# The low part of q padded with zero rows, so that both score matmuls of a head have 128 rows of weights

## The chip, the cores and the metric

The kernel runs on one core of one Trainium2 chip. The metric is device time in microseconds, the median of several runs. Three engines' names recur below: TensorE (PE in the profile) does matmuls and transposes, VectorE (DVE) and ScalarE (ACT) do elementwise work and read PE's results from the eight PSUM banks, GpSimd (POOL) does elementwise work on SBUF, and SyncE (SP) issues most DMAs.

## What is computed

Three layers in float32, one after the other, over 2304 tokens (4 sequences of 576) of 512 features:

```python
# attention: 8 heads of 64, each query sees its own and the 63 keys before it
scores = np.matmul(q, k.transpose(0, 1, 3, 2)) / np.sqrt(64)
rel = pos[:, None] - pos[None, :]
scores = np.where((rel >= 0) & (rel < 64), scores, -1e9)
attn = softmax(scores)                       # exp of scores less their maximum, over the sum + 1e-9
x = np.matmul(attn, v)                       # then [tokens, 512]
# feed-forward: d_ff 1536
xn = x / np.sqrt(np.mean(x * x, -1) + 1e-6) * rms_g
g = xn @ w_gate
x = (g * sigmoid(g) * (xn @ w_val)) @ w_out
# mixture of 8 experts, one for each token: 512 -> 1024 -> 512
e = argmax(x @ r_gate);  gate, eom = softmax(x @ r_gate)[e], sigmoid(x @ r_eom)[e]
out = gate * eom * (relu(x @ w1[e]) @ w2[e])
```

## The kernel before

**Numbers in two parts.** TensorE runs in a fast float32 form that rounds its operands. To keep precision every operand is split into a rounded part and the rest ("high" and "low", written by the helpers `hi_i` and `lo_i`, for q with its scale by `scaled_hi` and `scaled_lo`), and a product is the sum of high x high, high x low and low x high, accumulated in one bank. So a feed-forward step has three matmuls for each block of weights (lines 1117 to 1119 for gate and value, 1159 to 1161 for the output).

**Tiles and stages.** The tokens are 18 tiles of 128. For a tile, `attention_front` loads q, k and v, turns q and k with TensorE (line 578) and splits them; `attention_tile` computes the scores in two halves of four heads, adds the mask on VectorE (line 775), takes the maximum (787), the exponential on ScalarE (791), normalises (`nm`: 808 on ScalarE, else 357), turns the probabilities with TensorE (824), multiplies with v (880), and normalises the rows. The feed-forward layer takes the tiles in six groups (of 4, 2, 3, 3, 3 and 3 tiles); in the plan the attention of one group stands beside the feed-forward work of the group before. The experts follow at the end.

**What sets the order.** Each operation is given to a planner (`Plan`) with its engines' estimated costs, what it reads and writes, and a due time (`prio`). Its list scheduling picks for each engine the next operation and, where several engines could do it, the engine. It also models TensorE's clock: work of a low weight `rows` counts less towards keeping it up. The outcome is one fixed order for every engine; a cost that is changed can so move other instructions.

**Scores of the later tiles.** From tile 7 on (`K["stk"]`, 11 tiles), q and k are stacked. A head has 64 features, and heads go in pairs: head 2i lies in partitions 0 to 63 and head 2i+1 in partitions 64 to 127 of what the transposes leave. For the heads of one parity j, `stack(qb, j)` is a block of 128 partitions with the high part of q twice, and `stack(kt, j)` one with the high part of k in the half that is the head's own and the low part in the other. One matmul of 128 rows (line 758) so gives high x high and high x low together. The remaining low x high is a second matmul into the same columns of the bank (line 759) that uses only the head's own 64 partitions of both operands. The low part of q stands in the third block of `q_all`, even heads in the upper half of the partitions, odd heads in the lower. An operation (`mm`) does two heads, hence four matmuls of 192 columns; a tile has four of them, 16 matmuls, and the 11 tiles 176.

**Tile 0 to 6** use another form (`mmz`, lines 729 to 731): q is laid out with zeros, all its matmuls have 128 rows, and `q_all` is filled with zeros once at the start (line 562).

Of the kernel before, what the change touches and what calls it, by code (L numbers as in the profile page):

```python
# [9 lines left out]
F32 = mybir.dt.float32  # L10
# [29 lines left out]


class Buf:
    """An instance of a tag's tile: it takes one of the tag's slots from its first operation to its last."""

    def __init__(self, tag=None, t=None):
        self.tag, self.t, self.slot = tag, t, None
# [11 lines left out]


class Filler:  # L60
    """Work that keeps the tensor engine's clock up while it has none of its own."""

    def __init__(self, fn, lo):
        self.fn, self.lo = fn, lo


class Plan:
    """Operations with what they read and write, put in an order for every engine by list scheduling."""

    def __init__(self):  # L70
        self.ops, self.tags, self.ordered, self.newest, self.gates = [], {}, {}, {}, []
# [43 lines left out]
    def order(self):  # L115
# [21 lines left out]
        ticks = {}  # L137

        def pe_time(at, c, rows):
            """PE's time for c us of work at the full clock: a tick runs at half of it unless the one before was busy"""  # L140
            t0 = at
            while c > 1e-9:
                n = int(at / TICK + 1e-9)
                rate = 1.0 if ticks.get(n - 1, 0.0) >= FULL else 0.5
                step = min(c / rate, (n + 1) * TICK - at + 1e-9)
                c -= step * rate
                at += step
                ticks[n] = ticks.get(n, 0.0) + step * rate * rows
            return at - t0
# [18 lines left out]
        while left:  # L168
            while wait and wait[0][0] <= now + 1e-9:
                t, _, e, o = heapq.heappop(wait)  # L170
# [99 lines left out]
def attention_ffn_moe(  # L270
# [115 lines left out]
            yield done, step, b, s  # L386
            done += step

# [1 line left out]
    tag("t2k", "r", 2, [P, XW])  # L390
    ident = fixed("ident", [P, P])
    ones = fixed("ones", [P, 2])
# [16 lines left out]
        )  # L409

    def c_masks(e):
        """rows: 64 queries, twice; columns: their window's 128 keys; variants: inside, at the start of a batch, inside, inside"""
        nc.gpsimd.memset(masks.t, 0.0)
        for j in range(2):
            m = masks.t[64 * j:64 * j + 64]
            nc.gpsimd.affine_select(
                out=m, in_=m, compare_op=ALU.is_gt, fill=NEG, base=0, pattern=[[0, 4], [1, P]], channel_multiplier=-1
            )
            nc.gpsimd.affine_select(
                out=m, in_=m, compare_op=ALU.is_ge, fill=NEG, base=64, pattern=[[0, 4], [-1, P]], channel_multiplier=1  # L420
            )
        nc.gpsimd.memset(masks.t[:, 1, 0:64], NEG)
# [46 lines left out]
        nc.sync.dma_start(out=rw.t[:, :, E:2 * E], in_=r_eom.rearrange("(k p) e -> p k e", p=P))  # L469


# [1 line left out]
    tag("bank", "ps", 8, [P, 512])  # L473
    tag("raw", [("r", 3), ("mr", 3)], 0, [P, 2 * DM], I32)
    tag("rx", "a", 4, [P, DM])
# [35 lines left out]
    for us in GROUPS:  # L511
        GT.append(GT[-1] + PP * sum(SIZES[u] for u in us))

# [1 line left out]
    attn_ops = []  # L515

    def bank():
# [7 lines left out]
    xn_w, xn_r = [[] for _ in SIZES], [[] for _ in SIZES]  # L525

    def vt(t):
        """where tile t's attention stands in the plan"""
        g = GROUP[UNIT[t][0]]
        if g == 0:  # L530
            return t * K["stag"]
        first = FT[GROUPS[g][0]]
        n = FT[GROUPS[g][-1] + 1] - first
        return GT[g - 1] + (t - first) * (GT[g] - GT[g - 1]) / n * K["span"] - K["lead"]
# [8 lines left out]
        return go  # L543

    def low(t, bk, b, h, l, prio, sc=False):
        """what the rounded parts (b, 0) leave of the bank, into (b, 1)"""
        def v():
            return bk.t.rearrange("p (i t) -> p i t", t=P)

        pl.op(  # L550
            cost(512, "lp"), lambda e: (scaled_lo if sc else lo_i)(e, l(), v(), h()), r=[bk, (b, 0)], w=[(b, 1)],
            prio=prio,
        )

    kt_b = {}
    qb = Buf(None, q_all[:, 0:3 * DM].rearrange("p (z i t) -> p z i t", z=3, i=4))
    qz = q_all.rearrange("p (z i c t) -> p z i c t", z=2, i=4, c=2)

    def zeros(e):
# [7 lines left out]
    def attention_front(t):  # L567
# [21 lines left out]
            return slice(64 * j, 64 * j + 64)  # L589

        def stack(b, j, w=None):
            """the block of the heads of parity j in a stacked tile, as [partitions, pairs, columns]"""
            n = 192 if w else P
            a = b.t[:, 0:2].rearrange("p z i t -> p (z i t)").rearrange("p (i j t) -> p i j t", j=2, t=n)[:, :, j]
            return a[:, :, w] if w else a

        if t < K["qzt"]:
            for j in range(2):
                def own(z, j=j):
                    return qz[half(j), z, :, :, half(j)]  # L600

                def turned(bk=bk, j=j):
                    return bk.t[half(j)].rearrange("p (i c t) -> p i c t", i=4, c=2)

                pl.op(
                    cost(512, "hp"), lambda e, own=own, turned=turned: scaled_hi(e, own(0), turned()),
                    r=[bk], w=[(qb, (j, 0))], prio=pr,
                )
                pl.op(
                    cost(512, "lp"), lambda e, own=own, turned=turned: scaled_lo(e, own(1), turned(), own(0)),  # L610
                    r=[bk, (qb, (j, 0))], w=[(qb, (j, 1))], prio=pr,
                )
        elif not stk:
            pl.op(cost(512, "hp"), lambda e, bk=bk: scaled_hi(e, qb.t[:, 0], view(bk)), r=[bk], w=[(qb, 0)], prio=pr)
            low(t, bk, qb, lambda: qb.t[:, 0], lambda: qb.t[:, 1], pr, sc=True)
        else:
            for j in range(2):
                a, z = half(j), half(1 - j)
                pl.op(
                    cost(512, "hp"), lambda e, bk=bk, j=j, a=a: scaled_hi(e, stack(qb, j)[a], view(bk)[a]),  # L620
                    r=[bk], w=[(qb, (j, 0))], prio=pr,
                )
                pl.op(
                    cost(512, "hs"), lambda e, j=j, a=a, z=z: hi_i(e, stack(qb, j)[z], stack(qb, j)[a]),
                    r=[(qb, (j, 0))], w=[(qb, (j, 1))], prio=pr, lock="pv",
                )
                pl.op(
                    cost(512, "lp"), lambda e, bk=bk, j=j, a=a: scaled_lo(e, qb.t[a, 2], view(bk)[a], stack(qb, j)[a]),
                    r=[bk, (qb, (j, 0))], w=[(qb, (j, 2))], prio=pr,
                )  # L630
        bk2 = bank()
# [48 lines left out]
    def attention_tile(t, kt, rv, stack):  # L680
# [30 lines left out]
        for hf in range(2):  # L711
# [36 lines left out]
            for j in range(0 if zt else 2):  # L748
                bk = bank()

                def mm(e, bk=bk, hf=hf, j=j):
                    sv = bk.t[:, 0:384].rearrange("p (h w) -> p h w", w=192)
                    r = slice(64 * j, 64 * j + 64)
                    for i in range(2):
                        pr_ = 2 * hf + i
                        if t >= K["stk"]:
                            kk = stack(kt, j, slice(0, 192))[:, pr_]
                            nc.tensor.matmul(sv[:, i], lhsT=stack(qb, j)[:, pr_], rhs=kk, start=True, stop=False)  # L758
                            nc.tensor.matmul(sv[:, i], lhsT=qb.t[r, 2, pr_], rhs=kk[r], start=False, stop=True)  # L759
                            continue  # L760
                        qh, ql = (qb.t[r, z, pr_] for z in range(2))
                        kh, kl = (kt.t[r, z, pr_] for z in range(2))
                        nc.tensor.matmul(sv[:, i], lhsT=qh, rhs=kh, start=True, stop=False)
                        nc.tensor.matmul(sv[:, i], lhsT=qh, rhs=kl, start=False, stop=False)
                        nc.tensor.matmul(sv[:, i], lhsT=ql, rhs=kh, start=False, stop=True)

                pl.op(
                    {"t": 0.41 if t >= K["stk"] else 0.62}, mm, r=[qb, kt], w=[bk], hold=[s], prio=ps_, rows=0.45,
                )

                def mask(e, bk=bk, j=j, s=s):
# [59 lines left out]
            low(t, bk, pb, lambda pb=pb: pb.t[:, 0], lambda pb=pb: pb.t[:, 1], pp_)  # L831

        def kept(hf, z, h, c):
            """the probabilities of head h of half hf for the queries of chunk c, turned"""
            a = pb_[hf].t[:, z]
            i, j = divmod(h, 2)
            return a[..., 2 * i + c, 64 * j:64 * j + 64] if zt else a[..., h, 64 * c:64 * c + 64]
# [141 lines left out]
        ))  # L979
        attn_ops.append(xn_w[p_][-1])  # L980

# [1 line left out]
    wch = {}  # L983
    step = (GT[1] - GT[0]) / NF

# [196 lines left out]
            pl.op({"a": 0.48, "v": 0.6}, ev, r=[acc[j]], w=[(x2[p, j], 0)], prio=pr + 1)  # L1182
            pl.op({"v": 0.07}, ev2, r=[tok, (x2[p, j], 0)], w=[(x2[p, j], 1)], prio=pr + 1.1)

# [1 line left out]
    def small(nm, shape, dt=F32):  # L1186
        return [const.tile(shape, dt, name=f"{nm}{i}", bufs=1) for i in range(2)]

# [138 lines left out]

    nop_t = [const.tile([1, 1], F32, name="nop", bufs=1)]

# [1 line left out]
    TILES = [-(-c // P) for c in CAPS]  # L1331
    NIT = NTILE - min(TILES) + E
    mc = max(TILES)
# [188 lines left out]
    ew = {}  # L1522

    def weights(w, ch, hf, pr):
        """half a chunk of expert w's weights: loaded, split, held as [hi/lo, 2, 512]"""
        a, b = Buf("raw"), Buf("w")
        ew[w, ch, hf] = b

# [26 lines left out]
    first_loads = []  # L1555

    def tokens(b, j, pr):
        """tile j of block b: its rows loaded and turned"""
        a = Buf("t2k" if b < 1 else "xs")
        if j == 0:  # L1560
            xt_b[b] = Buf("fx" if b < 0 else "xT")
# [38 lines left out]
    puts = []  # L1600

    def narrow(b, w, pr):
        """relu(x @ w1) of a block of one tile, with the tokens stationary"""
        x = xt_b[b]
        hs = []
        for ch in range(2):
# [31 lines left out]
        return hs  # L1638

    def wide(b, w, N, pr):  # L1640
        """relu(x @ w1) of a block, with the weights stationary"""
        x = xt_b[b]
        hs = []
        c1 = 12 * max(N, 256) / 2400 + 0.03
# [69 lines left out]
        return pr  # L1714

    def experts(tt0):
        """every block's work with its time in the plan"""
        blocks = [(-1, 0, FIRST * P)] + [(b, b, CAPS[b]) for b in range(E)]
        at = tt0
        todo = []  # L1720
# [80 lines left out]
                in_=o, in_offset=None, bounds_check=NT - 1, oob_is_err=False,  # L1801
            )

# [1 line left out]
    for t in range(NTILE):  # L1805
        attention_front(t)
    for g in range(len(GROUPS)):
# [60 lines left out]
```

## Time and profile before

| | |
|---|---|
| time, median of 3 runs | 930.96 us (928.19 to 932.77) |
| the profiled execution | span 933.0 us from its first to its last instruction; no time around it is given |
| instructions | 16213 |
| TensorE, matmuls | 910.7 us busy, 98% of the span |
| TensorE, loads of weights (PEld) | 826.6 us, 89% |
| VectorE | 596.7 us, 64% |
| ScalarE | 392.7 us, 42% |
| GpSimd | 250.9 us, 27% |
| mean granted clock of TensorE | 0.974 of full speed |

How to read it: a matmul's duration in the profile runs to a modelled end and overlaps the next one, so a busy TensorE is not TensorE at its peak. What a matmul costs in a row of matmuls is the time from its start to the start of the next. The granted clock (PEclk) is the share of full speed that TensorE was allowed in a stretch. An idle time is put down to what ended it.

### The profile page before, as it was taken

Reading aid. Unit: us, or ns where it says so; the run is one execution under the profiler, and the core shown is the slowest. Engines: PE = TensorE matmul, PEld = TensorE weight load, DVE = VectorE, ACT = ScalarE, POOL = GpSimd, SP = SyncE. Lnnn points to the kernel's source line nnn. Section 1 sums busy time; section 2 is a strip of 40 time slices with the busy share of each in tenths; the row PEclk is TensorE's granted clock in tenths of the full one; section 3 lists DMA queues with packets and bytes.
Section 4 is the critical chain, followed back from the end, with each engine's and each line's share of the span. In section 5 each row is a group of like instructions: output and inputs, shape, how many; then the busy total and the mean of one; then the engine's idle time right before and its main releaser. Section 6 shows DMA issues by size and latency. Waiting matters only on the chain.

```text
span 933.0 us, 16213 instructions
## 1 busy us (share of the span) xinstructions
PE 910.7 (98%) x5820; PEld 826.6 (89%) x5820; DVE 596.7 (64%) x1397; ACT 392.7 (42%) x1040; POOL 250.9 (27%) x427
## 2 busy tenths in 40 slices
PE   8999999999999999999999999999999999999996
PEld 8998989999889889899898898999997888989995
DVE  6699779965775665586646756455567544746650
ACT  6798568643344332264313533211235232433331
POOL 5676351321022221042112320110012223323310
PEclk9799999999999989899998999999999999999999
DMA  9977899647344350384304531672029443556600
GB/s 230 239 205 214 274 271 281 211 138 258 113 125 143 130 157 13 91 221 141 102 12 119 176 136 46 260 248 91 1 94 373 149 163 112 184 191 218 213 24 24
DMA packets 114706, 149.01 MB, mean 160 GB/s; under 512 B 62752, under 2 KB 75040, under 8 KB 114624
## 3 DMA queue, kind: packets, MB, share of 16 engines
q1 hardware_dynamic: 111536, 137.84, 48.8%
q0 software_dynamic: 3088, 10.11, 2.9%
q8 instruction: 47, 0.77, 0.3%
q14 instruction: 35, 0.29, 0.1%
HBM read 113.96 MB, written 24.80 MB: 149 GB/s over the span
## 4 chain that ended last, share of the span: by engine, by line
PE 81%; DVE 5%; DMA 4%; issue 4%; ACT 3%; POOL 2%; SPq 0%; POOLq 0%; DVEq 0%; ACTq 0%
PE bank L1117 11%; PE bank L1118 10%; PE bank L1119 10%; PE bank L1159 5%; PE bank L1160 5%; PE bank L1161 5%; PE bank L1655 3%; PE bank L1657 3%; PE bank L1656 3%; PE bank L1690 3%; PE bank L1691 3%; PE bank L1689 3%; PE bank L759 3%; PE bank L758 3%; PE bank L880 2%
## 5 line engine op out<-in xcount | busy, mean ns | idle before, releaser
L1117 PE MATMUL bank<-xn,w 128*128 128x384 f32 (+1 forms) x672 | 219.7, 327 | 4.5 <-DVE p L354 1.4
L1118 PE MATMUL bank<-xn,w 128*128 128x384 f32 (+1 forms) x672 | 213.5, 318 | 0.0
L1119 PE MATMUL bank<-xn,w 128*128 128x384 f32 (+1 forms) x672 | 213.3, 317 | 0.0
L1117 PEld LDWEIGHTS bank<-xn,w 128*128 128x128 f32 x672 | 129.8, 193 | 9.3 <-DVE u L1134 1.7
L1118 PEld LDWEIGHTS bank<-xn,w 128*128 128x128 f32 x672 | 129.9, 193 | 1.8
L1119 PEld LDWEIGHTS bank<-xn,w 128*128 128x128 f32 x672 | 129.6, 193 | 0.0
L1129 ACT ACTIVATE u<-bank 128x384 f32<-128x384 f32 (+1 forms) x84 | 37.3, 444 | 163.6 <-PE bank L1119 146.0
L1159 PE MATMUL bank<-wo,h 128*128 128x512 f32 x216 | 88.8, 411 | 0.0
L1161 PE MATMUL bank<-wo,h 128*128 128x512 f32 x216 | 86.1, 398 | 0.0
L1160 PE MATMUL bank<-wo,h 128*128 128x512 f32 x216 | 85.8, 397 | 0.0
L1142 DVE TENSOR_TENSOR u<-u,bank 128x384 f32<-128x384 f32 (+1 forms) x84 | 41.5, 494 | 54.8 <-PE bank L1119 53.3
L1134 DVE SCALAR_TENSOR_TENSOR u<-u,bank 128x384 f32<-128x384 f32 (+1 forms) x84 | 41.6, 495 | 50.7 <-ACT u L1129 50.2
L354 DVE TENSOR_TENSOR w<-raw,w 128x512 fp32r<-128x512 f32 x106 | 71.9, 712 | 0.0
L351 DVE CAST w<-raw 128x512 fp32r<-128x512 f32 x55 | 27.7, 531 | 66.0 <-PE bank L1691 54.5
L1655 PE MATMUL bank<-xT,w 128*128 128x256 f32 (+2 forms) x224 | 69.3, 310 | 0.0
L1656 PE MATMUL bank<-xT,w 128*128 128x256 f32 (+2 forms) x224 | 69.3, 309 | 0.0
L1657 PE MATMUL bank<-xT,w 128*128 128x256 f32 (+2 forms) x224 | 69.3, 309 | 0.0
L1689 PE MATMUL bank<-w,eh 128*128 128x512 f32 (+1 forms) x168 | 66.8, 397 | 0.0
L1690 PE MATMUL bank<-w,eh 128*128 128x512 f32 (+1 forms) x168 | 66.3, 395 | 0.0
L1691 PE MATMUL bank<-w,eh 128*128 128x512 f32 (+1 forms) x168 | 66.3, 395 | 0.0
L357 POOL TENSOR_TENSOR y<-y 128x1 f32<-128x1 f32 x126 | 33.2, 264 | 114.4 <-ACT y L935 105.6
L1661 ACT ACTIVATE eh<-bank 128x256 fp32r<-128x256 f32 (+2 forms) x64 | 27.6, 431 | 67.9 <-PE bank L1657 65.2
(273 smaller groups left out, 2040.6 us busy)
## 6 DMA issues: line engine op xcount, KB each, us to landing
w<-whd SPq DMA_DIRECT2D x80, 512.0 KB, 4.3
raw<-in_moe_w_dram SPq DMA_DIRECT2D x64, 512.0 KB, 5.0
whd<-w SPq DMA_DIRECT2D x24, 512.0 KB, 5.2
vof<-val SPq DMA_DIRECT2D x35, 256.0 KB, 3.8
raw<-in_moe_w_gate_dram SPq DMA_DIRECT2D x12, 512.0 KB, 5.0
raw<-in_moe_w_val_dram SPq DMA_DIRECT2D x12, 512.0 KB, 4.7
raw<-in_moe_w_out_dram SPq DMA_DIRECT2D x12, 512.0 KB, 5.2
xs<-xs SPq DMA_DIRECT2D x17, 257.0 KB, 3.2
```

What stands on the lines that cost most here:

```text
L1117: nc.tensor.matmul(o, lhsT=h_, rhs=xn.t[:, 0, kk], start=(kk == 0), stop=False)
L1118: nc.tensor.matmul(o, lhsT=h_, rhs=xn.t[:, 1, kk], start=False, stop=False)
L1119: nc.tensor.matmul(o, lhsT=l_, rhs=xn.t[:, 0, kk], start=False, stop=(kk == KD - 1))
L1159: nc.tensor.matmul(o, lhsT=h.t[:, 0, c], rhs=wo.t[:, 0, f], start=(n == 0), stop=False)
L1160: nc.tensor.matmul(o, lhsT=h.t[:, 0, c], rhs=wo.t[:, 1, f], start=False, stop=False)
L1161: nc.tensor.matmul(o, lhsT=h.t[:, 1, c], rhs=wo.t[:, 0, f], start=False, stop=(n == NF - 1))
L1655: nc.tensor.matmul(o, lhsT=wh, rhs=x.t[:, 0, kk, 0:N], start=(kk == 0), stop=False)
L1656: nc.tensor.matmul(o, lhsT=wh, rhs=x.t[:, 1, kk, 0:N], start=False, stop=False)
L1657: nc.tensor.matmul(o, lhsT=wl, rhs=x.t[:, 0, kk, 0:N], start=False, stop=(kk == KD - 1))
L1689: nc.tensor.matmul(bk.t[0:M], lhsT=hh, rhs=wh, start=(f == 0), stop=False)
L1690: nc.tensor.matmul(bk.t[0:M], lhsT=hh, rhs=wl, start=False, stop=False)
L1691: nc.tensor.matmul(bk.t[0:M], lhsT=hl, rhs=wh, start=False, stop=(f == NF2 - 1))
```

## The change

The low part of q of odd heads gets a block of its own, the fourth of `q_all`. The third block holds the low part of even heads in partitions 0 to 63 and zeros in 64 to 127; the fourth holds zeros in 0 to 63 and the low part of odd heads in 64 to 127. The zeros are written once, by two memsets on GpSimd at tile 7 (before it the space belongs to the other form). The second matmul of a head takes all 128 rows of its block and the whole stacked block of k; the rows with the low part of k meet zeros. The planner is told 0.45 instead of 0.41 us for an operation of four such matmuls, and the weight `rows` goes from 0.45 to 0.75. Comments and docstrings fall away, and lines from 616 on move down by 6.

```diff
-    qb = Buf(None, q_all[:, 0:3 * DM].rearrange("p (z i t) -> p z i t", z=3, i=4))
+    qb = Buf(None, q_all.rearrange("p (z i t) -> p z i t", z=4, i=4))
...
         else:
+            if t == K["stk"]:
+                def blank(e):
+                    for j in range(2):
+                        nc.gpsimd.memset(qb.t[half(1 - j), 2 + j].bitcast(F32), 0.0)
+
+                pl.op({"p": 1.1}, blank, w=[(qb, "blank")], prio=pr)
             for j in range(2):
...
-                    cost(512, "lp"), lambda e, bk=bk, j=j, a=a: scaled_lo(e, qb.t[a, 2], view(bk)[a], stack(qb, j)[a]),
+                    cost(512, "lp"), lambda e, bk=bk, j=j, a=a: scaled_lo(e, qb.t[a, 2 + j], view(bk)[a], stack(qb, j)[a]),
...
                             nc.tensor.matmul(sv[:, i], lhsT=stack(qb, j)[:, pr_], rhs=kk, start=True, stop=False)
-                            nc.tensor.matmul(sv[:, i], lhsT=qb.t[r, 2, pr_], rhs=kk[r], start=False, stop=True)
+                            nc.tensor.matmul(sv[:, i], lhsT=qb.t[:, 2 + j, pr_], rhs=kk, start=False, stop=True)
...
-                    {"t": 0.41 if t >= K["stk"] else 0.62}, mm, r=[qb, kt], w=[bk], hold=[s], prio=ps_, rows=0.45,
+                    {"t": 0.45 if t >= K["stk"] else 0.62}, mm, r=[qb, kt], w=[bk], hold=[s], prio=ps_, rows=0.75,
```

TensorE has the same instructions before and after, and most of its order is the same. One place where it differs is the scores of tile 8. Before, after the transpose that belongs to a norm (line 961), its 16 score matmuls stand in one run; its start:

```order
L961 MATMUL bank_3653<-ident,y_3589 128x128
L758 MATMUL bank_3655<-kt_2406,q_all 128x192
L759 MATMUL bank_3655<-kt_2406,q_all 128x192
L758 MATMUL bank_3655<-kt_2406,q_all 128x192
L759 MATMUL bank_3655<-kt_2406,q_all 128x192
L758 MATMUL bank_3665<-kt_2406,q_all 128x192
```

After (lines 764 and 765 are 758 and 759 of before, 1165 to 1167 are 1159 to 1161):

```order
L967 MATMUL bank_3661<-ident,y_3586 128x128
L764 MATMUL bank_3663<-kt_2430,q_all 128x192
L765 MATMUL bank_3663<-kt_2430,q_all 128x192
L764 MATMUL bank_3663<-kt_2430,q_all 128x192
L765 MATMUL bank_3663<-kt_2430,q_all 128x192
L1165 MATMUL bank_3205<-wo,h_3631 128x512
L1166 MATMUL bank_3205<-wo,h_3631 128x512
L1167 MATMUL bank_3205<-wo,h_3631 128x512
L1165 MATMUL bank_3206<-wo,h_3631 128x512
L1166 MATMUL bank_3206<-wo,h_3631 128x512
L1167 MATMUL bank_3206<-wo,h_3631 128x512
L764 MATMUL bank_3682<-kt_2430,q_all 128x192
```

Six output matmuls have moved between the first four score matmuls and the other twelve.

On GpSimd the two memsets come into its queue at tile 7. Before, behind the splits of earlier feed-forward work, the old keys of tile 7 are copied for tile 8 (`kt`), and splits of feed-forward weights (`w`) follow:

```order
L354 TENSOR_TENSOR h_2333<-u_2307,h_2333 128x256
L354 TENSOR_TENSOR w_2198<-t_2301,w_2198 128x512
L349 TENSOR_SCALAR kt_2406<-kt_1461 128x8x64
L349 TENSOR_SCALAR w_2410<-t_2476 128x512
L349 TENSOR_SCALAR w_2560<-t_2561 128x512
```

After:

```order
L354 TENSOR_TENSOR h_2333<-u_2307,h_2333 128x256
L354 TENSOR_TENSOR w_2198<-t_2301,w_2198 128x512
L620 MEMSET q_all 64x512 x2
L349 TENSOR_SCALAR kt_2430<-kt_1461 128x8x64
L349 TENSOR_SCALAR w_2410<-t_2492 128x512
```

The memsets stand ahead of the copy and of the splits; nothing else changes its place there.

## The prediction

> **What bounds the kernel now.** I read the page first: the busy shares and the chain that ended last.
>
> ```profile
> PE 910.7 (98%) x5820; PEld 826.6 (89%) x5820; DVE 596.7 (64%) x1397; ACT 392.7 (42%) x1040; POOL 250.9 (27%) x427
> ...
> PE 81%; DVE 5%; DMA 4%; issue 4%; ACT 3%; POOL 2%; SPq 0%; POOLq 0%; DVEq 0%; ACTq 0%
> ```
>
> TensorE is busy 98% of the span and carries 81% of the chain. Then busy time by stage: the first row holds every attention tile that the change touches (score matmuls from 160.3 to 564.5), the second the stage without attention.
>
> ```profile
> 143.00:570.00 427.00, 424.26 (x2620) 381.70 (x2619) 289.93 (x706) 177.13 (x508) 92.19 (x196) 0.96 0.47 141
> 570.00:928.00 358.00, 353.02 (x2023) 318.36 (x2021) 194.26 (x476) 108.25 (x223) 75.18 (x79) 1.00 0.44 153
> ```
>
> After the stretch come PE, PEld, DVE, ACT and POOL busy, granted clock, DMA share, GB/s. In the attention stage PE has 2.7 us free of 427, VectorE 137, and the clock is below full. So a microsecond taken from PE there is worth a microsecond until another engine is late. The instructions that change, by line:
>
> ```profile
> L758 PE MATMUL bank<-kt,q_all x88: 247/355/528, 160.3 to 564.5; 128*128 128x192 f32 x88
> ...
> L759 PE MATMUL bank<-kt,q_all x88: 350/352/526, 160.6 to 564.8; 64*128 64x192 f32 x88
> ```
>
> Durations of matmuls overlap and mislead; what a matmul costs is the step from its start to the next start. So I read the timeline, first around tile 8, whose sixteen score matmuls stand in one run (eight L758 and eight L759, alternating):
>
> ```profile
> 236.78 0.28 PE L1118 MATMUL bank<-xn,w 128*128 128x256 f32 x1
> 236.90 0.28 PE L1119 MATMUL bank<-xn,w 128*128 128x256 f32 x1
> ...
> 237.04 0.33 PE L758 MATMUL bank<-kt,q_all 128*128 128x192 f32 x1
> 237.31 0.35 PE L759 MATMUL bank<-kt,q_all 64*128 64x192 f32 x1
> ...
> 241.29 0.35 PE L759 MATMUL bank<-kt,q_all 64*128 64x192 f32 x1
> 241.57 0.39 PE L1117 MATMUL bank<-xn,w 128*128 128x256 f32 x1
> ```
>
> Sixteen steps from 237.04 to 241.57 are 4.53 us, 0.283 each, after 128-row and after 64-row matmuls alike. A feed-forward matmul with a third more columns (256) steps in 0.12. The early tiles have score matmuls whose weights have 128 rows throughout, from the same tensors and accumulating in the same way:
>
> ```profile
> 141.54 0.28 PE L729 MATMUL bank<-kt,q_all 128*128 128x128 f32 x1
> 141.65 0.28 PE L730 MATMUL bank<-kt,q_all 128*128 128x128 f32 x1
> ```
>
> They step in 0.11. What is particular to the slow ones is the alternation of 64 and 128 rows: each change costs some 0.17 us, with PE "busy" only by its modelled ends.
>
> Next the clock. These are the stretches of score matmuls and the stretch behind each:
>
> ```profile
> 237.00:242.20 5.20, 5.20 (x24) 3.60 (x23) 4.87 (x13) 1.02 (x2) 0.73 (x1) 1.00 0.87 277
> 242.20:245.60 3.40, 3.40 (x14) 3.01 (x14) 2.18 (x5) 1.60 (x8) 0.00 (x0) 0.51 0.00 0
> 275.50:279.80 4.30, 4.25 (x15) 2.77 (x15) 3.93 (x17) 1.31 (x3) 1.00 (x1) 1.00 0.66 246
> 279.80:283.20 3.40, 3.40 (x11) 3.22 (x11) 2.63 (x6) 1.72 (x3) 2.39 (x5) 0.50 0.10 37
> ...
> 337.50:341.20 3.70, 3.70 (x15) 2.29 (x14) 3.59 (x7) 0.60 (x2) 1.27 (x1) 1.00 0.86 260
> 341.20:348.00 6.80, 6.80 (x17) 5.42 (x18) 5.14 (x13) 3.26 (x16) 0.63 (x1) 0.50 0.27 60
> 387.20:389.00 1.80, 1.80 (x8) 1.20 (x8) 0.98 (x4) 0.92 (x3) 0.71 (x1) 1.00 0.00 1
> 389.00:395.80 6.80, 6.80 (x18) 5.13 (x19) 3.56 (x15) 0.00 (x0) 0.58 (x2) 0.50 0.36 77
> 449.70:453.90 4.20, 4.20 (x17) 2.68 (x15) 3.36 (x8) 0.51 (x1) 1.00 (x1) 1.00 0.68 250
> 453.90:457.30 3.40, 3.40 (x11) 3.23 (x12) 1.55 (x4) 0.00 (x0) 0.00 (x0) 0.50 0.00 0
> 497.80:501.70 3.90, 3.90 (x16) 2.58 (x15) 2.76 (x13) 0.92 (x3) 1.29 (x2) 0.99 0.10 22
> 501.70:508.50 6.80, 6.80 (x22) 6.05 (x22) 2.95 (x14) 1.54 (x7) 0.00 (x0) 0.50 0.30 64
> ```
>
> Every run of score matmuls shown here is followed by 3.4 or 6.8 us at half clock, 30.6 us together; half of that, 15.3 of 427 us, is all that the stage's clock of 0.96 lacks to 1.00. The runs are also the thinnest work that PE has there: 15 matmuls in 4.3 us against 2620 in 427.
>
> **The change part by part.** *Score steps.* 176 matmuls change (88 of each line); after it all have 128 rows. No row shows 128 rows with 192 columns in a row; the bounds are 0.11 (128 columns) and 0.12 (256 columns). I take 0.112, nearer the lower: the step per column above 256 (0.12 to 0.17 for 384 columns, rows below) would put 192 columns under 0.11, so what holds the 128-column step should hold this. In half-clock stretches the step is longer:
>
> ```profile
> 389.15 0.53 PE L759 MATMUL bank<-kt,q_all 64*128 64x192 f32 x1
> ...
> 392.80 0.53 PE L759 MATMUL bank<-kt,q_all 64*128 64x192 f32 x1
> 393.26 0.69 PE L1117 MATMUL bank<-xn,w 128*128 128x384 f32 x1
> ...
> 394.06 0.52 PE L1119 MATMUL bank<-xn,w 128*128 128x384 f32 x1
> 394.38 0.52 PE L1117 MATMUL bank<-xn,w 128*128 128x384 f32 x1
> ...
> 396.29 0.33 PE L1118 MATMUL bank<-xn,w 128*128 128x384 f32 x1
> 396.46 0.34 PE L1119 MATMUL bank<-xn,w 128*128 128x384 f32 x1
> ```
>
> Nine steps in 4.11 us: 0.457. The timeline has 14 such steps (none, 1, 2, 9, none and 2 in the six stretches), so 162 are at full clock. Saved: 162 x (0.283 - 0.112) = 27.7 us and 14 x (0.457 - 0.112) = 4.8 us, together 32.5; with 0.12 it is 31.1.
>
> *The clock.* The half-clock stretches hold 30.6 - 14 x 0.457 = 24.2 us of other work, feed-forward mostly, at 0.32 a step instead of 0.17 (394.06 to 394.38, 396.29 to 396.46). If the clock stays up this saves 24.2 x (1 - 0.17/0.32) = 11.3 us. A run of sixteen then lasts 1.8 us with a matmul every 0.112, as dense as the feed-forward work around it (0.12 and 0.17), which keeps the clock. I take the whole 11.3; the lower end is 0.
> The Trainium skill (TensorE: Matmul & The Clock Gate, section HAM oscillation) gives the rule that the clock falls on gaps of PE of more than some 3.4 us. By the rows ahead of the six PE is busy throughout (5.20 of 5.20, 4.25 of 4.30), so by that rule the drops would have another cause and stay, and the sum would lack the 11.3. The rows put a run of score matmuls ahead of each, so I don't follow it; its outcome is rival 1.
>
> *Rows of zeros.* Two GpSimd memsets of 64x512, once, at tile 7. Two of double the size at the start show the price; GpSimd's queue stands idle soon behind their place:
>
> ```profile
> L562 POOL MEMSET q_all<- x2: 941/944/946, 1.3 to 2.3; 64x1024 f32 x2
> ...
> 151.63 0.62 POOL L349 TENSOR_SCALAR w<-t 128x512 fp32r<-128x512 f32 x1 [7.20 <-DVE t L1036]
> ```
>
> So 0.95 us in all. Queued behind them is the copy of tile 8's old keys, read by PE only from 237.04, and then the split at 151.63, which waits 7.2 us for VectorE anyway: cost 0. Were that cover gone, 0.95. The low parts of q go to a second block for odd heads: same instructions, same sizes, 0. The loads of weights grow from 64 to 128 rows; their step is inside the 0.112.
>
> *The order.* The plan counts a group of four at 0.45 instead of 0.41, so orders shift a little: tile 8's run of sixteen is cut by six feed-forward matmuls, a few copies move between ScalarE, VectorE and GpSimd, and a few loads swap places on SP's queue. No row prices that. All of PE's free time in the stage is 2.7 us, so I bound it by -2 and +2 us and take 0, between them.
>
> *What is late next.* Without the waits of PE, its followers have less time. The run at tile 14:
>
> ```profile
> 449.65 0.25 PE L758 MATMUL bank<-kt,q_all 128*128 128x192 f32 x1
> ...
> 450.79 0.86 DVE L775 TENSOR_TENSOR s<-bank,masks 64x256 f32<-64x256 f32 x2 [0.24 <-PE bank L759]
> ...
> 454.67 0.86 DVE L775 TENSOR_TENSOR s<-bank,masks 64x256 f32<-64x256 f32 x2
> ...
> 460.49 0.69 DVE L357 TENSOR_TENSOR s<-s,m 128x512 f32<-128x512 f32 x1
> ...
> 462.00 0.60 PE L824 MATMUL bank<-ident,s 128*128 128x128 f32 x4
> ```
>
> VectorE masks in pairs of 0.86 behind each bank, from 450.79 to 455.53, 4.7 us with its other work. PE would deliver in 1.8, so VectorE ends only some 0.6 us sooner, while PE is 2.7 us sooner, and VectorE becomes the late one. But PE has gate, value and output matmuls in between (12 x 0.17 = 2.1 us for a gate group) before it needs the probabilities, which today lie ready at 461.18, 0.8 us ahead of 462.00. Where the advance of 2.7 us eats this slack, up to 1.9 us a tile would be lost. I put the new waits at 0.4 us for each of the 11 tiles, 4.4, since PE stands for 2.7 us in all there today; lowest 0, highest 1.5 a tile, 16, as not every tile is this close.
>
> Sum: 32.5 + 11.3 - 4.4 = 39.4 us. The profiled execution has a span of 933.0, so 893.6 for it; nothing is shown around the span, and the median of the runs, 930.96, lies 2.0 below it. From the median: 891.6, and I forecast 892.
>
> **The rivals.** (1) *The clock still drops* behind the shorter runs: only 32.5 - 4.4 = 28 us, 903. For it: drops of 6.8 us outlast the run, so feed-forward work in them didn't end them at once. Against: the step of 0.112 is as dense as work that keeps the clock.
> (2) *VectorE gives much back*: 16 us of waits, 903; with half of the clock's part lost too, 909. For it: the 0.8 us of slack at tile 14 and VectorE's 290 busy of 427. Against: its 137 free.
> (3) *No change*: 0.283 belongs to 192 columns, not to 64 rows; 931. For it: no 192-column row without the alternation. Against: 128 and 256 columns both step in 0.12 or less.
> (4) *Slower*: PE outruns VectorE so far that it stands idle and the clock halves once for every tile. A halved 3.4 us costs 3.4 x 0.47 = 1.6; it decides from 43.8/11 = 4.0 us lost per tile on, that is 2.4 us of standing besides; at 5 us a tile it is 942. Against: all of PE's free time in the stage is 2.7 us.
> The Trainium skill (TensorEngine Tiling (Array Packing), Theoretical Speedup) says that matmuls over 64 rows or fewer can run two at once, up to twice as fast, so padding would throw that away: were the 88 low matmuls overlapped today, 88 x 0.112/2 = 5 us slower, 936. The rows show L759 to L758 at 0.283, so nothing overlaps; the same page (Tiling Modes, Key Properties) says that a change of tiling mode drains the engine, which agrees with 0.283 against 0.11.
>
> **How the numbers follow.** My forecast (885 to 899) 0.77; clock stays low 0.08; much given back 0.10; no change 0.03; slower 0.02. All but the last two are over 0.5% faster: 0.95; 0.5%, 4.7 us, is about what a measurement of this kernel can tell. The low end, 884, is the sum without any wait (43.8 off: 887) with 2 us of order and 1 of the runs' spread; the high end, 907, takes in rivals 1 and most of 2.
>
> **What would show it.** Steps right: score matmuls at 0.11 from start to start. Clock: no half-clock stretch between 143 and 530, PEclk in that stage 0.99 or more. Cover: the memsets near 144 with no wait of PE on GpSimd. Waits: PE's idle time before the transposes of probabilities (line 824 before) and before gate matmuls on masks, 2 to 7 us. Wrong if the score step is over 0.15, if half-clock stretches remain, or if these waits pass 12 us.

## The result, and the profile after

The changed kernel takes 897.62 us (median; 893.65 to 898.51) against 930.55 us for the kernel before: a ratio of 0.9626, 95% interval 0.9577 to 0.9675, 32.9 us less. A second session gave 897.35 us and 0.962 (0.9587 to 0.9653). The profiled execution took 897.01 us with a span of 895.3.

The page's busy shares and the chain that ended last:

```profile
PE 869.3 (97%) x5820; PEld 803.4 (90%) x5820; DVE 598.7 (67%) x1407; ACT 395.3 (44%) x1039; POOL 242.1 (27%) x420
...
PE 76%; DVE 7%; issue 6%; DMA 4%; ACT 3%; POOL 2%; SPq 0%; POOLq 0%; DVEq 0%; ACTq 0%
```

TensorE still bounds the kernel, a little less. The changed line and a run of sixteen score matmuls, tile 14's, by line and in the timeline of TensorE:

```profile
L765 PE MATMUL bank<-kt,q_all x88: 272/274/278, 160.0 to 527.3; 128*128 128x192 f32 x88
```

```profile
427.01 0.25 PE L764 MATMUL bank<-kt,q_all 128*128 128x192 f32 x1
427.09 0.28 PE L765 MATMUL bank<-kt,q_all 128*128 128x192 f32 x1
...
428.66 0.27 PE L765 MATMUL bank<-kt,q_all 128*128 128x192 f32 x1
428.77 0.36 PE L1123 MATMUL bank<-xn,w 128*128 128x384 f32 x1
```

From 427.09 to 428.77 there are fifteen steps, 0.112 each; the run takes 1.76 us where tile 8's took 4.53. Then the stages (stretch; PE, PEld, DVE, ACT, POOL busy; granted clock; DMA share; GB/s): the attention stage, now 143 to 535, the stage behind it, and two short stretches:

```profile
143.00:535.00 392.00, 385.83 (x2635) 360.80 (x2634) 293.38 (x718) 181.48 (x514) 83.74 (x189) 1.00 0.51 153
535.00:893.00 358.00, 350.15 (x2006) 315.66 (x2004) 192.76 (x473) 106.02 (x214) 74.28 (x79) 1.00 0.43 153
262.90:266.40 3.50, 2.32 (x20) 2.22 (x19) 3.41 (x8) 1.60 (x4) 1.19 (x1) 0.99 1.24 250
266.40:269.80 3.40, 3.40 (x12) 3.40 (x12) 2.83 (x11) 1.40 (x4) 0.00 (x0) 0.50 0.61 102
```

The attention stage is 35 us shorter, its clock 1.00 where it was 0.96. One half-clock stretch of 3.4 us is left of 30.6, and it doesn't follow scores: TensorE had just waited 1.2 us for VectorE at the routing. TensorE's free time in the stage rose from 2.7 to 6.2 us. Behind it nothing changed: from the end of the last score run (565.0 before, 527.4 now) to the end of the span it is 368 us in both.

### The profile page after: what moved, and what is told of

Read it like the earlier page. It is cut to its first block, busy times and chain, and to the rows that moved or that the text cites. A ratio compares the mean times of both kernels' runs of the same rounds, so it can differ in the third digit from the quotient of the medians.

```text
span 895.3 us, 16213 instructions
## 1 busy us (share of the span) xinstructions
PE 869.3 (97%) x5820; PEld 803.4 (90%) x5820; DVE 598.7 (67%) x1407; ACT 395.3 (44%) x1039; POOL 242.1 (27%) x420
## 4 chain that ended last, share of the span: by engine, by line
PE 76%; DVE 7%; issue 6%; DMA 4%; ACT 3%; POOL 2%; SPq 0%; POOLq 0%; DVEq 0%; ACTq 0%
PE bank L1123 10%; PE bank L1125 10%; PE bank L1124 10%; PE bank L1165 5%; PE bank L1167 5%; PE bank L1166 5%; PE bank L1661 3%; PE bank L1663 3%; PE bank L1662 3%; PE bank L1696 3%; PE bank L1695 3%; PE bank L1697 3%; PE bank L886 3%; PE bank L830 1%; DMA xs<-raw,si 1%
## 5 line engine op out<-in xcount | busy, mean ns | idle before, releaser
L1123 PE MATMUL bank<-xn,w 128*128 128x384 f32 (+1 forms) x672 | 215.2, 320 | 4.1 <-DVE u L1140 1.5
L1125 PE MATMUL bank<-xn,w 128*128 128x384 f32 (+1 forms) x672 | 211.1, 314 | 0.0
L1124 PE MATMUL bank<-xn,w 128*128 128x384 f32 (+1 forms) x672 | 210.8, 314 | 0.0
L1123 PEld LDWEIGHTS bank<-xn,w 128*128 128x128 f32 x672 | 127.8, 190 | 6.7 <-DVE u L1140 1.7
L1124 PEld LDWEIGHTS bank<-xn,w 128*128 128x128 f32 x672 | 127.8, 190 | 1.6
L1125 PEld LDWEIGHTS bank<-xn,w 128*128 128x128 f32 x672 | 127.5, 190 | 0.0
L1165 PE MATMUL bank<-wo,h 128*128 128x512 f32 x216 | 87.2, 404 | 0.0
L1167 PE MATMUL bank<-wo,h 128*128 128x512 f32 x216 | 85.1, 394 | 0.0
L1166 PE MATMUL bank<-wo,h 128*128 128x512 f32 x216 | 84.9, 393 | 0.0
```

Of the source, the lines that this page charges most:

```text
L1123: nc.tensor.matmul(o, lhsT=h_, rhs=xn.t[:, 0, kk], start=(kk == 0), stop=False)
L1124: nc.tensor.matmul(o, lhsT=h_, rhs=xn.t[:, 1, kk], start=False, stop=False)
L1125: nc.tensor.matmul(o, lhsT=l_, rhs=xn.t[:, 0, kk], start=False, stop=(kk == KD - 1))
L1165: nc.tensor.matmul(o, lhsT=h.t[:, 0, c], rhs=wo.t[:, 0, f], start=(n == 0), stop=False)
L1166: nc.tensor.matmul(o, lhsT=h.t[:, 0, c], rhs=wo.t[:, 1, f], start=False, stop=False)
L1167: nc.tensor.matmul(o, lhsT=h.t[:, 1, c], rhs=wo.t[:, 0, f], start=False, stop=(n == NF - 1))
```

## The experiments

Theory A says that the price is at each change between matmuls of 64 and 128 rows, and that runs of such thin work halve the clock. Rival B gives a good part to the new order of instructions. Rival C holds 64-row matmuls slow in themselves.

**The planner's numbers apart.** The first kernel has the padding with the old numbers; TensorE's order is then that of the kernel before, row for row. The second has the new numbers without the padding; TensorE's order is that of the changed kernel.

```diff
 changed kernel, e1
-                    {"t": 0.45 if t >= K["stk"] else 0.62}, mm, ... rows=0.75,
+                    {"t": 0.41 if t >= K["stk"] else 0.62}, mm, ... rows=0.45,
 kernel before, e2
-                    {"t": 0.41 if t >= K["stk"] else 0.62}, mm, ... rows=0.45,
+                    {"t": 0.45 if t >= K["stk"] else 0.62}, mm, ... rows=0.75,
```

> The changed kernel with the planner's old numbers (0.41 us, rows 0.45), so that TensorE's order is that of the kernel before, word for word. Theory A (the price is at each change between 64 and 128 rows, and the runs of such thin work halve the clock): steps of the score matmuls 0.12 us, at most one half-clock stretch, 897 us, 893 to 901. Rival B (a good part comes from the new order that the new numbers make): 905 to 920.

> The kernel before with the planner's new numbers alone (0.45 us, rows 0.75): TensorE's order of the changed kernel, but the low matmuls with 64 rows. Theory A: steps of 0.283 us as before, half-clock stretches as before but perhaps not the one behind tile 8, whose run is cut in two: 929 us, 925 to 933. Rival B: 905 to 920.

Measured: padding alone 893.28 us, ratio 0.9562 (0.9494 to 0.9630); numbers alone 938.1 us, 1.0066 (1.0026 to 1.0105). The padding gives all of the gain and the order none; rival B fell. The second kernel is above what I expected: the new order seems to cost something. Its profiled execution, its fastest (931.88 us), has four half-clock stretches in the attention stage, 20.5 us together, and none behind tile 8, whose run is cut in two. By matmul line of the two, durations with 128 and with 64 rows:

```profile
L765 PE MATMUL bank<-kt,q_all x88: 272/274/278, 163.5 to 529.8; 128*128 128x192 f32 x88
```

```profile
L759 PE MATMUL bank<-kt,q_all x88: 350/352/526, 160.6 to 561.6; 64*128 64x192 f32 x88
```

With the numbers alone the low matmuls keep their 0.352, and 0.526 at half clock. With the padding they never reach half clock. But the trace with the padding alone, of the slowest of its four executions (899.38 us), has two half-clock stretches where I expected one at most:

```profile
139.60:146.40 6.80, 6.80 (x28) 6.22 (x27) 5.04 (x10) 6.00 (x12) 4.34 (x6) 0.50 0.96 268
265.90:272.70 6.80, 5.92 (x18) 5.93 (x19) 5.19 (x19) 3.34 (x8) 0.00 (x0) 0.50 0.42 97
```

Neither follows a run of the changed matmuls. The first comes ahead of all of them, 1.2 us after a wait of TensorE of 1.78 us; the second begins in a wait of 1.18 us at the routing.

**Fewer changes without padding.** The order of an operation's four matmuls is high, low, low, high.

```diff
 kernel before
-                            nc.tensor.matmul(sv[:, i], lhsT=stack(qb, j)[:, pr_], rhs=kk, start=True, stop=False)
-                            nc.tensor.matmul(sv[:, i], lhsT=qb.t[r, 2, pr_], rhs=kk[r], start=False, stop=True)
+                            if i == 0:
+                                nc.tensor.matmul(sv[:, i], lhsT=stack(qb, j)[:, pr_], rhs=kk, start=True, stop=False)
+                            nc.tensor.matmul(sv[:, i], lhsT=qb.t[r, 2, pr_], rhs=kk[r], start=i == 1, stop=i == 0)
+                            if i == 1:
+                                nc.tensor.matmul(sv[:, i], lhsT=stack(qb, j)[:, pr_], rhs=kk, start=False, stop=True)
```

> The kernel before with the four score matmuls of an operation in the order high, low, low, high, so that the two 64-row matmuls stand side by side and the 128-row ones of neighbouring operations do: two changes of rows where there were four, nothing padded. Theory A: of the four steps two stay at 0.283 and two (low to low, and high to the next high) fall to 0.11 to 0.12: 88 x 0.165 = 14.5 us less, a run of sixteen lasts 3.2 us instead of 4.5, and part of the 11 us of the clock comes back: 908 to 916. Rival C (a 64-row matmul is slow in itself, whatever its neighbours): the step from low to low stays at 0.283, and at most 44 steps fall: 7 us, 922 to 926.

Measured: 913.0 us, 0.9777 (0.9690 to 0.9864), inside theory A's range. The steps by matmul starts surprised me: all four are near 0.2. The start that is recorded for the first matmul behind a change is that of its own weight load, so the loads are the better clock. TensorE's weight loads in the run of tile 11 (759 and 762 high, 760 low):

```profile
332.31 0.29 PEld L760 LDWEIGHTS bank<-kt,q_all 64*128 64x128 f32 x2 [0.21 <-issue]
332.70 0.19 PEld L762 LDWEIGHTS bank<-kt,q_all 128*128 128x128 f32 x1
332.81 0.19 PEld L759 LDWEIGHTS bank<-kt,q_all 128*128 128x128 f32 x1
333.10 0.29 PEld L760 LDWEIGHTS bank<-kt,q_all 64*128 64x128 f32 x2
333.50 0.19 PEld L762 LDWEIGHTS bank<-kt,q_all 128*128 128x128 f32 x1
```

High to high, 332.70 to 332.81, is 0.11. High to low, 332.81 to 333.10, is 0.29. Two low loads side by side take 0.29 together, one of 0.19 and a step of 0.10 to 0.11; the next high load comes 0.29 behind the second. So the price sits at the load behind a change, in either direction: it starts 0.29 behind the load ahead of it, where a load without a change starts 0.11 behind. That it waits there for the matmul ahead to leave the array is my reading; the ends of matmuls are modelled and don't show it. Rival C fell: low to low is a normal step. The Trainium skill (TensorEngine Tiling (Array Packing), Tiling Modes, Key Properties) says that a change of tiling mode drains the engine; these rows agree, with some 0.18 us for one change.

**Half of the padding.** Zero rows for even heads alone, with the old numbers.

```diff
 changed kernel
-                    for j in range(2):
-                        nc.gpsimd.memset(qb.t[half(1 - j), 2 + j].bitcast(F32), 0.0)
+                    nc.gpsimd.memset(qb.t[half(1), 2].bitcast(F32), 0.0)
...
-                            nc.tensor.matmul(sv[:, i], lhsT=qb.t[:, 2 + j, pr_], rhs=kk, start=False, stop=True)
+                            rr = r if j else slice(0, P)
+                            nc.tensor.matmul(sv[:, i], lhsT=qb.t[rr, 2 + j, pr_], rhs=kk[rr], start=False, stop=True)
```

> The changed kernel with the zero rows for even heads alone and the planner's old numbers; odd heads' low matmuls keep 64 rows. Half of the operations alternate. Theory A: the same number of changes as with the four matmuls grouped, so the same direct part, 14.5 us; runs of sixteen last 3.2 us, so again part of the clock's 11 us: 908 to 916. That the zeros cost something in themselves (waits on the memsets, longer loads) would show as 917 or more.

Measured: 903.39 us, 0.9672 (0.9606 to 0.9737), faster than my range. The direct part came in both: the score steps sum to 34.0 us here and to 36.3 with grouping, 17.7 and 15.5 under the 51.8 before, where I had put 14.5. What I missed is the clock. The attention stage (143 to 600) here, and then the one of the kernel with four matmuls grouped:

```profile
143.00:600.00 457.00, 454.07 (x2968) 418.67 (x2968) 318.39 (x798) 192.21 (x544) 100.55 (x215) 1.00 0.51 156
```

```profile
143.00:600.00 457.00, 454.46 (x2943) 419.38 (x2944) 316.69 (x792) 190.99 (x543) 100.39 (x214) 0.98 0.49 151
```

Here the clock is whole, 1.00, where grouping leaves 0.98, though a run of sixteen at full clock is hardly shorter (3.1 to 3.2 us in both). The other executions agree: the mean clocks of the four are 0.987 to 0.996 here and 0.975 to 0.988 with grouping. Where the two meet, 907.29 us at 0.987 here and 906.78 at 0.988 there, the times are nearly equal. So the direct part goes by the number of changes, which is the same, and the difference between the two is the clock's. Why the clock fell more with grouping isn't shown. In its trace half-clock stretches begin in or behind two of the seven runs of sixteen; a third follows a wait of TensorE of 1.25 us at the routing, and here a wait of 1.27 us at the same place has none behind it.

**64 rows throughout.** The stacked form is never used, and a head's three products are three matmuls of 64 rows.

```diff
 changed kernel
-    qzt=7, spe=4, lact=12, warm=50, wf=1.17, flead=36.7, pvt=5, stk=7, nwp=18, ...
+    qzt=7, spe=4, lact=12, warm=50, wf=1.17, flead=36.7, pvt=5, stk=18, nwp=18, ...
```

> The changed kernel with the stacked form never used (stk 18): every head of tiles 7 to 17 has its three products as three matmuls of 64 rows, in the upper or lower half of the partitions. 264 matmuls of 64 rows instead of 176 of 128, no change of rows inside a run of scores, less copying of q and k. Theory A: the step of 64-row matmuls among themselves is 0.11 to 0.12, as that of 128-row ones, 0.28 only at both ends of a run; scores cost 264 x 0.115 = 30 us and 4 to 6 us for the ends, against 21 now: 903 to 911, if the clock stays up. If the clock goes by rows in use and not by the gaps, dense 64-row runs of 16 to 24 lower it too: 911 to 920, with half-clock stretches behind them. Rival C (64 rows are slow in themselves): steps of 0.2 or more, 930 or more.

Measured: 905.48 us, 0.9722 (0.9682 to 0.9763), as theory A has it. A run of one operation in TensorE's timeline, and the place where a run in one half of the rows meets one in the other half:

```profile
333.31 0.27 PE L770 MATMUL bank<-kt,q_all 64*128 64x192 f32 x1
333.43 0.27 PE L771 MATMUL bank<-kt,q_all 64*128 64x192 f32 x1
333.54 0.27 PE L769 MATMUL bank<-kt,q_all 64*128 64x192 f32 x1
333.65 0.28 PE L770 MATMUL bank<-kt,q_all 64*128 64x192 f32 x1
```

```profile
331.50 0.28 PE L771 MATMUL bank<-kt,q_all 64*128 64x192 f32 x1
331.50 0.38 PE L769 MATMUL bank<-kt,q_all 64*128 64x192 f32 x2
331.70 0.29 PE L770 MATMUL bank<-kt,q_all 64*128 64x192 f32 x2
331.81 0.30 PE L771 MATMUL bank<-kt,q_all 64*128 64x192 f32 x2
```

64 rows step in 0.11 among themselves: they aren't slow. The clock stays up behind nearly all such runs (0.99 in the attention stage): of its two half-clock stretches one follows a wait of TensorE of 2.2 us, away from scores, and one begins at the end of a run that held a wait of 0.4. So few rows alone don't halve it. That the standing between the matmuls does is the reading that is left; no view here measures it. And where two halves meet, two matmuls start at once.

**The order again.** The kernel with the old numbers and the changed kernel once more, in one session.

> The changed kernel with the planner's old numbers once more, beside the changed kernel in the same session, to settle whether the new order costs something. Theory A2 (the padding gives all, and the order that the new cost of 0.45 makes takes some 5 us back, by a wait of 2 us of TensorE before the routing's transposes near 210 us and two shorter ones): 0.5% faster than the changed kernel, some 893. Rival (chance, by where the half-clock stretches fall): the two agree within 0.3%.

> The changed kernel itself, in the same session. Theory A2: 898, 0.5% above the one with the old numbers, with the wait near 210 us again. Rival: within 0.3% of it.

Measured: 895.62 us, 0.9592 (0.9556 to 0.9629), with the old numbers, and 897.35 us, 0.962 (0.9587 to 0.9653), with the new. The difference of 0.2% is inside both intervals: inconclusive by itself, and nearer the rival's mark (within 0.3%) than my 0.5%. It has the same sign between the two first measurements (0.9562 against 0.9626) and in the numbers alone (1.0066). The wait that I named is there in the changed kernel. VectorE, ScalarE and TensorE near 210 us:

```profile
211.13 0.60 ACT L1181 ACTIVATE raw<-bank 128x512 f32<-128x512 f32 x1 [6.05 <-DMA xs<-raw,si]
211.62 0.38 ACT L1135 ACTIVATE u<-bank 128x256 f32<-128x256 f32 x1
212.03 0.42 DVE L1140 SCALAR_TENSOR_TENSOR u<-u,bank 128x256 f32<-128x256 f32 x1 [0.81 <-ACT u L1135]
212.51 0.66 PE L1233 MATMUL bank<-ident,raw 128*128 128x128 f32 x4 [2.20 <-DVE u L1140]
```

ScalarE waits 6 us for a scatter of routed rows to land and free a buffer, VectorE waits for ScalarE, and TensorE for a bank. The new order puts this copy ahead of the gate's work there; with the old order this wait of TensorE is absent. From 143 us to the last score matmul TensorE stands 6.2 and 5.3 us in the two traces of the changed kernel, and 4.1 in both with the old numbers.

Executions at the same mean clock separate this from the clock. At 0.985 the old numbers took 896.53 and 897.28 us and the new ones 898.20; at 0.984 it was 898.85 and 900.83. Without the padding, at 0.970, the kernel before took 936.41 to 937.92 and the one with the new numbers 938.10. So my estimate is that the order itself costs some 1 to 2 us, and that the rest of the differences goes with the clock. The two can hang together: in the second trace of the changed kernel a half-clock stretch of 3.4 us begins at 213.41, 0.5 us behind this wait.

**Two halves in turn.** The overlap pointed to another version: no stacking, and the 64-row products of an even and an odd head issued in turn, into two banks.

```diff
 changed kernel, stk=18; the two operations of a half become one
+                    for i in range(2):
+                        pr_ = 2 * hf + i
+                        for zq, zk in ((0, 0), (0, 1), (1, 0)):
+                            for j in range(2):
+                                r = slice(64 * j, 64 * j + 64)
+                                nc.tensor.matmul(
+                                    sv[j][:, i], lhsT=qb.t[r, zq, pr_], rhs=kt.t[r, zk, pr_],
+                                    start=zq == zk == 0, stop=zq == 1,
+                                )
+                pl.op({"t": 0.82}, mm, r=[qb, kt], w=bks, hold=[s], prio=ps_, rows=0.75)
```

> The changed kernel without the stacked form, and with the three 64-row products of an even and an odd head issued in turn, into two banks: upper half, lower half, upper half. Where two runs of 64-row matmuls of different halves met in the run with 64 rows alone, their steps ran side by side. Theory D (matmuls in different halves of the rows overlap in full): 24 matmuls of a tile take 12 steps of 0.112, 1.3 us against 1.8 with padding, so scores cost 15 us and some 3 us for the ends of the runs, 18 against 20.5; with less copying of q and k on ScalarE and VectorE: 891 to 898. Rival E (they overlap only in part, the weights being loaded one after the other): 24 steps of 0.11, as in the run with 64 rows alone: 903 to 911.

Measured: 890.12 us, 0.9541 (0.9499 to 0.9583), the lowest median of all, just under my range of 891 to 898, and 0.8% under the changed kernel by the ratios. Its interval lies just below that of the changed kernel in the second session (0.9587 to 0.9653), but overlaps that of the padding with the old numbers (0.9556 to 0.9629). A whole tile's scores in TensorE's timeline:

```profile
321.35 0.34 PE L1119 MATMUL bank<-xn,w 128*128 128x384 f32 x1
321.62 1.58 PE L764 MATMUL bank<-kt,q_all 64*128 64x192 f32 x24
323.13 0.44 PE L1117 MATMUL bank<-xn,w 128*128 128x384 f32 x1
```

24 matmuls take 1.51 us from the first start to the next work: twelve steps of 0.11, and some 0.2 more at the ends, where the rows change. The steps of all 264 sum to 17.5 us, where the 176 padded ones sum to 21.3. The Trainium skill (TensorEngine Tiling (Array Packing), Theoretical Speedup) promises up to a factor of two for 64 rows; inside this run it is met, with two matmuls that start 3 to 4 ns apart in each step. How much of the gain is the steps, how much the copies that fall away (ScalarE 371.2 us busy against 395.3, VectorE 579.4 against 598.7) and how much another order wasn't taken apart.

## Why the prediction was right

The direction, the mechanism and the size held: 892 forecast, 897.6 measured, in the range of 884 to 907. Term by term, from the two profiled executions:

- *Score steps.* Forecast 32.5 us less, with 0.112 a step. The step is 0.112; the sum of the 176 steps fell from 51.8 to 21.3 us, 30.5 less. It is 2 us short because the steps before had a mean of 0.280 at full clock, the first of a run being shorter, and because the steps now sum to 1.6 us more than 176 of 0.112; 1.2 of that lie in two long steps (1.09 and 0.31 us), the first with a wait of 0.8.
- *The clock.* Forecast 11.3. One stretch of 3.4 us remains and costs 1.6, so 9.7 came. The prediction had named half-clock stretches that remain as a sign of being wrong, and one did. But rival 1 had the wrong cause: no short run of scores is followed by a drop. In the four traces in which all low matmuls are padded, six half-clock stretches begin between 139 and 535 us, none of them in or behind a run of scores. Before, one began in or behind six of the seven runs of sixteen; the seventh, at 560.6, has none, nor have the shorter runs. So the drops at scores went with the alternation, though not every run of it brought one. By the rule of gaps (the Trainium skill, TensorE: Matmul & The Clock Gate, HAM oscillation) that the prediction set aside they would have stayed, since the profile shows TensorE busy ahead of each; the array can still have stood in the drains, which a modelled busy time doesn't show, so whether gaps inside the runs were what counted is open.
- *What is late next.* Forecast 4.4; TensorE's free time rose by 3.4. The sum was near, the place was not: 2.2 us are the wait at 212.51, which is the new order's, and the waits on masks are small. VectorE does end later than TensorE, as I said; its masks of tile 14:

```profile
427.81 2.63 DVE L781 TENSOR_TENSOR s<-bank,masks 64x256 f32<-64x256 f32 x6
430.48 0.69 DVE L793 TENSOR_REDUCE m<-s 128x4 f32<-128x512 f32 x1
431.19 0.86 DVE L781 TENSOR_TENSOR s<-bank,masks 64x256 f32<-64x256 f32 x2
```

  They end at 432.05, 3.3 us behind the run (1.3 before), and the feed-forward matmuls between cover it: no wait of TensorE is recorded from 426 to 437.
- *The order.* Taken as 0, between -2 and +2. It seems to cost something: 0.2 to 0.7% by three comparisons, 2 to 6 us, of which only that of the numbers alone has an interval that excludes no change (1.0026 to 1.0105). At the same granted clock it is 1 to 2 us, inside my bounds but not 0; what goes beyond is the clock, which I didn't count here. I argued from TensorE's small free time before and not from what the moved instructions wait for.
- *Rows of zeros.* The memsets took 0.52 us each, 1.1 together, at 143.43, and the split behind them at 151.63 still waited 6.5 us for VectorE: 0, as forecast.

The wait of 0.8 us in a score step stands in two of the terms; 30.5 + 9.7 - 3.4 + 0.8 is 37.6 us, and the spans differ by 37.7. The forecast of 892 took the saving off a median of 930.96, 2.0 under the span. The profiled execution now shows 1.7 us around its span, so the profiled execution before was some 4 us longer than the median of its kernel, and the difference of the two spans is larger than that of the medians (32.9). This is most of what lies between 892 and 897.6: the terms were read off an execution slower than the median that they were taken from, and only 1.7 us (39.4 forecast against 37.7) are errors of the terms, in sum. Rival 4, slower, came nowhere near. The rival of overlapping 64-row matmuls was rightly refuted for the kernel before, where 128-row matmuls stand between them, but the overlap itself exists.

## What to carry to other kernels

Where matmuls of fewer rows stand between matmuls of 128, read the starts of the weight loads: if the load behind each change starts late (0.29 us behind the one ahead here, not 0.11), pay for the rows with zeros, which cost nothing here, or group the small ones; if they can be paired in different halves of the rows and different banks, that may be better still, as in the last experiment. Look at the granted clock in and behind such runs, since they cost a second time there in this kernel. And a planner's number that is corrected moves other instructions: time the correction apart.

## What was not expected of the hardware

- The clock fell with no wait of TensorE over 0.3 us on record in the 7 us ahead: in or behind six of seven runs of sixteen that alternated throughout (some 4.5 us at full clock), two of seven with four matmuls grouped (3.1 to 3.2 us), and none of seven with half of the padding (3.1 to 3.2 us). These are single traces; what exactly is counted stays open.
- The spread between executions of one kernel is largely the clock's: the kernel before took 925.75 us at a mean clock of 0.983 and 937.92 at 0.970, the changed one 893.65 at 0.992 and 900.83 at 0.984.
- Matmuls of 64 rows in different halves start together, and a pair of them costs one step of 0.11.
